# Expert 1's rows stay on the chip and its weights head SyncE's queue: a change to an mLSTM-and-routing kernel

## The chip, the cores and the metric

The kernel runs on one core of one Trainium2 chip. What counts is the device time of one execution in microseconds, as the median of several runs. Engines are named as in the profile: PE (TensorE matmul), PEld (its weight load), DVE (VectorE), ACT (ScalarE), POOL (GpSimd), SP (SyncE). SPq and POOLq are the DMA instructions that these engines issue; q1 is the DMA queue of SP's transfers, q0 that of POOL's.

## The reference

Two blocks follow each other. The first is an mLSTM cell over 4 batches, 8 heads, 768 time steps and head size 40. The second takes the result as 3072 rows of 320 numbers and sends each row through one of 8 experts, chosen by a hash of its token id:

```
for t in range(S):
    m_new = max(f_gate[t] + m, i_gate[t])
    f_stab, i_stab = exp(f_gate[t] + m - m_new), exp(i_gate[t] - m_new)
    C = f_stab * C + i_stab * outer(v[t], k[t]);  n = f_stab * n + i_stab * k[t]
    y[t] = sigmoid(o_gate[t]) * (C @ q[t]) / max(|n . q[t]|, 1)
x = y.transpose(0, 2, 1, 3).reshape(3072, 320)
expert_idx = token_ids * 2654435761 % 8
for e in range(8):
    rows = expert_idx == e
    out[rows] = relu(x[rows] @ w1[e]) @ w2[e]      # w1 320x1024, w2 1024x320
```

All data is float32.

## The kernel before, in words

**Attention stage** (until about 129 us). The 24 blocks of 128 rows are worked one after the other (the loop over `s`, L873). Meanwhile the routing tables are built: `g_idx` holds, for every expert, the numbers of the rows that it takes, `s_idx` where its results go. Each finished block of x is stored to a DRAM table `x_rows` (L585), the last ones from POOL's queue. Expert 0's weights are loaded in slices on SP's queue during the last blocks (`slices_of`, L120).

**Expert stage.** An expert takes 384 rows in three blocks (j = 0, 1, 2) and 32 remaining rows, 416 columns once turned. Its rows are gathered from `x_rows` by POOL's indirect DMA (`gather`, L109), turned so that the 320 features lie on partitions (`xT`: three blocks of features, the last one 64 wide and put there twice), multiplied by w1 with relu into `h` (layer 1) and by w2 into the result (layer 2), which ACT copies out of PSUM and POOL scatters to `out` (L980 to L993). The weights of one expert are `w1t` (256 x 1024), `w1c` (the last 64 rows of w1, folded) and `w2t`; `load_weights` (L116) issues them as four DMAs on SP.

*Expert 0* is written out plainly. `early_turn` (L807) turns its blocks 0 and 1 within the attention stage, and `layer1` (L142) makes h for these 256 columns at L970, in four rounds with two relus each: one on DVE (L165), one on ACT (L167). In the expert loop, `layer2` (L1107) follows for j = 0 and 1; between them PE turns the third block, `xg0[:, 2]` (`turn_third`), and inside j = 1 the remaining rows of experts 0 to 3 together, `xr0` (`turn_rest`). `turn` (L995) is two transposes, a 64-wide copy on DVE that doubles the last features (the pad, L1000), a third transpose, and a copy out of PSUM. Then layer 1 runs for the last 160 columns and layer 2 for j = 2.

*Experts 1 to 7* save one product in eight by sums: `sums_of_w1` (four DVE operations, `sw`), `sums_of_x` (`tx`), `differences_of_w2` (`tw`, on POOL), `sums_of_h` (`sh`). `layer1_by_seven` (PE lines L1060 and L1068) and `layer2_by_seven` (L1144) use them. Their rows are turned without PE: `fetch` gathers them into `xg`, SP writes that tile to a DRAM table `x_slots` (L1191; the remaining rows of four experts at L1198), `blocks` reads it back in twelve DMAs as 32-wide pieces (`xb`, L1206), and one DVE operation transposes the 32 x 32 squares (`turned`, L1210).

**What sets the order.** Every engine works its instructions in the order in which they are written, and so does SP's queue. Before the expert loop stand `fetch(0)`, `fetch(1)`, `blocks(1)`, `load_weights(1)`; in round e come `fetch(e+2)`, `blocks(e+2)`, `load_weights(e+2)` first. `sums_of_w1(W[e+1])` stands behind layer 2 of j = 2, for expert 0 too. The expert stage's tiles lie in memory that the attention stage's pools give back, so their first users wait for the last users of the old tiles.

Of the kernel before, what the change touches and what calls it, by code (L numbers as in the profile page):

```python
# [17 lines left out]
P = 128  # L18
# [4 lines left out]
def kernel(  # L23
# [85 lines left out]
    def gather(xg, idx, rows=N):  # L109
        nc.gpsimd.indirect_dma_start(  # L110
            out=xg, out_offset=None, in_=x_d[:rows, :], in_offset=bass.IndirectOffsetOnAxis(ap=idx, axis=0),
        )

    W = {}

    def load_weights(e, eng=None):  # L116

        W[e] = weights(moe_w1[e], moe_w2[e], wpools[e % 3 > 0], w2pools[e % 6 > 0], eng)
# [72 lines left out]
    with tc.tile_pool(name="gates", bufs=1) as gp, \  # L191
# [210 lines left out]
        def turn(s, what, tag="tr"):  # L402
            turned_in(s, what, tag)
            turned_out(s, what)
# [401 lines left out]

        def early_turn(j):  # L807
            tp = ps.tile([P, DB, P], F32, name="tpx", tag="tr", bufs=2)
            for db in range(DB):
                nc.tensor.transpose(tp[:, db, :], xg0[:, j, db * P : (db + 1) * P], ident[:])  # L810
            nc.scalar.copy(xT0[:, :, j * P : (j + 1) * P], tp[:])

        def unread(n):
# [59 lines left out]
        for s in range(NT):  # L873
# [76 lines left out]
                for j in range(2):  # L950
                    gather(xg0[:, j, :Dm], g_idx[:, j : j + 1], TE * P)
            if s == NT - 2:
                for j in range(2):
                    nc.vector.tensor_copy(xg0[:, j, Dm:], xg0[:, j, 2 * P : Dm])
                early_turn(0)
            if s == 2:
                g1.weights(kwT1)
# [19 lines left out]
    def psum():  # L977
        return mps.tile([P, 4 * P], F32, name="mh", bufs=8)
# [13 lines left out]
            tc.declare_no_dep(ins, group="rows_out", reason="disjoint rows")  # L992
            tc.add_to_no_dep_group("rows_out", ins)  # L993

    def turn(xg, dst, on_act):  # L995

        tp = psum().rearrange("p (d c) -> p d c", c=P)[:, :DB]
        for db in range(2):
            nc.tensor.transpose(tp[:, db, :], xg[:, db * P : (db + 1) * P], ident[:])
        nc.vector.tensor_copy(xg[:, Dm:], xg[:, 2 * P : Dm])  # L1000
        nc.tensor.transpose(tp[:, 2, :], xg[:, 2 * P :], ident[:])
        if on_act:
            nc.scalar.copy(dst, tp[:])
        else:
            nc.vector.tensor_copy(dst, tp[:])
# [169 lines left out]
    def cols_of(t, c0):  # L1175
        return lambda j: t[:, c0 + j : c0 + j + 1]

    with tc.manual_schedule():
        xTs, hrem, xbs = {}, {}, {}
        xr0 = xp.tile([P, DB * P], F32, name="xr0", bufs=1)  # L1180
        xTs[0] = xT0

        def fetch(e):
            if e == 0:
                gather(xg0[:, 2, :Dm], cols_of(g_idx, 0)(2))
                gather(xr0[:, :Dm], cols_of(g_idx, NR)(0))
            else:
                xg = xp.tile([P, NJ, Dm], F32, name="xg")
                for j in range(NJ):
                    gather(xg[:, j], cols_of(g_idx, e * NJ)(j))  # L1190
                nc.sync.dma_start(xs_d[e, :NM].rearrange("(t p) d -> p t d", p=P), xg[:])  # L1191
            if e % EG == 0:
                if e:
                    xr = xp.tile([P, Dm], F32, name="xrg", bufs=1)
                    gather(xr[:], cols_of(g_idx, NR + e // EG)(0))
                else:
                    xr = xr0[:, :Dm]
                nc.sync.dma_start(xs_d[e : e + EG, NM:], xr[:])  # L1198

        def blocks(e):  # L1200
            xb = xbs[e] = xp.tile([P, CAP // 32, DB, 32], F32, name="xb")
            rows = xs_d[e].rearrange("(g j) d -> j g d", j=32)
            for q in range(4):
                for c in range(DB):
                    d0 = c * P + (q if c + 1 < DB else q % 2) * 32
                    nc.sync.dma_start(xb[q * 32 : (q + 1) * 32, :, c], rows[:, :, d0 : d0 + 32])  # L1206
# [5 lines left out]
        def turn_third():  # L1212
            turn(xg0[:, 2], xT0[:, :, 2 * P : NM], False)

        def turn_rest():
            remT = xp.tile([P, DB, P], F32, name="remT", bufs=1)
            turn(xr0, remT[:], True)
            nc.gpsimd.tensor_copy(xT0[:, :, NM:], remT[:, :, :RM])

        def rest(g):  # L1220
            zp = psum()[:, :Dm]
# [5 lines left out]
                    )  # L1227
            scatter(zp, cols_of(s_idx, NR + g)(0), True)

        fetch(0)  # L1230
        fetch(1)
        blocks(1)
        load_weights(1)
        h = h0
        for e in range(E):
            g, i = e // EG, e % EG
# [4 lines left out]
            if i == 0:  # L1241
                hrem[g] = xp.tile([P, EG, FB, RM], F32, name="hrem")
            if e == 0:
                layer2(W[0], h, range(2), cols_of(s_idx, 0), True, lambda j: j == 0 and turn_third(), lambda j, fb: (j, fb) == (1, FB - 3) and turn_rest())
                layer1(W[0], xT0, h, 2 * P, CAP, bank)
                turned(1)
                tx = sums_of_x(xTs[1])
            else:
                tw = differences_of_w2(W[e])
                sh = xp.tile([P, 4, FB // 2, P], F32, name="sh", bufs=1)  # L1250
                layer1_by_seven(
                    W[e], sw, xTs[e], tx, h, lambda: 2 < e < E - 1 and turned(e + 1),
                    lambda g: sums_of_h(h, sh, g, nc.vector if g else nc.gpsimd),
                )
            nc.gpsimd.tensor_copy(hrem[g][:, i], h[:, :, NM:])
            layer2(W[e], h, (2,), cols_of(s_idx, e * NJ), True)
            if e + 1 < E:
                sw = sums_of_w1(W[e + 1])
            if i == EG - 1 and e + 1 < E:
                rest(g)  # L1260
# [62 lines left out]
```

## Time and profile before

| | |
|---|---|
| median of 3 runs | 354.02 us (353.84 to 356.44) |
| the profiled execution, its own time | 357.09 us |
| its span, from the first to the last profiled instruction | 355.3 us |
| mean granted TensorE clock | 0.98 |
| attention stage ends on PE | about 128.7 us |
| expert 0 ends on PE | about 159.0 us |
| expert 7's last PE work | about 345 us |
| HBM read and written | 46.28 MB and 12.38 MB |

A timeline row gives start, length, engine, line, operation, output<-inputs and a count; the bracket at its end is how long the engine stood idle before it and what ended that. A row of the windows view gives, for a stretch of time, its length, the busy time of PE, PEld, DVE, ACT and POOL, then the granted clock of PE (1.00 is full), the share of the DMA engines that was busy, and GB/s. Ends of PE rows are modelled, since matmuls overlap: a row's start to the next row's start is the better measure.

### The profile page before, as it was taken

How to read it: one execution, taken by the hardware profiler on the slowest of the kernel's cores; microseconds unless marked ns; L12 is line 12 of the kernel's file. 1: busy time of each engine (PE TensorE's matmuls, PEld its weight loads, DVE VectorE, ACT ScalarE, POOL GpSimd, SP SyncE). 2: the span in 40 equal slices, each digit the busy share in tenths (PEclk: the TensorE clock that was granted, in tenths of full speed). 3: DMA queues.
4: the chain of work that ended last, by engine and by line, in shares of the span. 5: the costliest groups of instructions: out<-in, count | busy, mean ns of one | idle time of the engine just before them, and what ended most of it. 6: DMA issues, size and time to landing. Idle time of an engine off the chain costs nothing.

```text
span 355.3 us, 10242 instructions
## 1 busy us (share of the span) xinstructions
PE 334.2 (94%) x4051; PEld 292.7 (82%) x4051; DVE 231.3 (65%) x542; ACT 130.0 (37%) x325; POOL 205.0 (58%) x316
## 2 busy tenths in 40 slices
PE   7799699999999899996999999999999999999993
PEld 6577588999988786766989899859989989899891
DVE  8977899888787851144576697745684785765610
ACT  4478656676656521110421411411321411411410
POOL 9562487987865317307444965942963946618512
PEclk9789999999999999998999999999999999999999
DMA  6599989898889974588697958768368477001001
GB/s 129 97 183 189 166 181 201 172 184 166 160 176 217 241 277 116 146 209 286 132 310 128 333 151 209 273 134 277 129 126 298 123 178 233 2 17 39 0 19 43
DMA packets 162871, 59.06 MB, mean 166 GB/s; under 512 B 140647, under 2 KB 158595, under 8 KB 162790
## 3 DMA queue, kind: packets, MB, share of 16 engines
q1 hardware_dynamic: 158854, 48.82, 59.5%
q0 software_dynamic: 2832, 9.34, 8.0%
q8 instruction: 33, 0.54, 0.6%
q10 hardware_dynamic: 1134, 0.21, 0.3%
q14 instruction: 18, 0.15, 0.1%
HBM read 46.28 MB, written 12.38 MB: 165 GB/s over the span
## 4 chain that ended last, share of the span: by engine, by line
PE 67%; DMA 9%; issue 6%; DVE 6%; POOL 6%; SPq 4%; ACT 1%; POOLq 0%; ACTq 0%; DVEq 0%
PE mh L1060 17%; PE mh L1144 13%; PE mh L1111 7%; PE xh L553 7%; PE mh L1068 5%; PE sp L480 5%; PE tr L413 4%; DMA og<-in_o_gate_dram 2%; DMA w1t<-in_moe_w_dram 2%; DMA x_slots<-xg 2%; SPq L1206 2%; PE ab L438 1%; PE xh L532 1%; PE mh L1224 1%; POOL out_dram L986 1%
## 5 line engine op out<-in xcount | busy, mean ns | idle before, releaser
L986 POOL DMA_INDIRECT out_dram<-zo,s_idx x26 | 26.5, 1021 | 71.2 <-issue 35.6
L1111 PE MATMUL mh<-w2t,h 128*128 128x320 f32 x160 | 45.0, 433 | 0.5 <-ACT h L167 0.5
L1111 PEld LDWEIGHTS mh<-w2t,h 128*128 128x128 f32 x160 | 30.0, 190 | 11.8 <-ACT h L167 0.9
L1046 DVE TENSOR_TENSOR h<-u,mh 128x416 f32<-128x416 f32 (+1 forms) x56 | 25.2, 476 | 17.0 <-PE mh L1068 6.2
L1060 PE MATMUL mh<-tx,sw 128*128 128x208 f32 x168 | 33.6, 352 | 1.0 <-DVE sw L1016 1.0
L1060 PEld LDWEIGHTS mh<-tx,sw 128*128 128x128 f32 x168 | 31.3, 199 | 1.4 <-DVE sw L1016 1.3
L110 POOL DMA_INDIRECT xg<-x_rows,g_idx x24 | 23.8, 990 | 13.0 <-issue 6.7
L1046 DVE TENSOR_TENSOR u<-m,mh 128x416 f32<-128x416 f32 x28 | 16.5, 588 | 19.7 <-PE mh L1060 16.5
L553 PE MATMUL xh<-v,w 128*64 128x41 f32 x384 | 27.5, 234 | 0.0
L1144 PE MATMUL mh<-tw,sh 128*128 128x160 f32 x168 | 27.4, 299 | 0.0
L496 DVE TENSOR_TENSOR w<-sp,w 128x384 f32<-128x384 f32 x48 | 24.5, 549 | 3.6 <-ACT w L442 3.6
L553 PEld LDWEIGHTS xh<-v,w 128*64 128x64 f32 x384 | 26.1, 145 | 0.0
L1060 PE MATMUL mh<-xT,w1t 128*128 128x208 f32 x112 | 23.2, 340 | 2.6 <-DMA w1t<-in_moe_w_dram 2.6
L480 PEld LDWEIGHTS sp<-qT,kT 40*64 40x64 f32 x960 | 20.2, 137 | 6.4 <-issue 5.0
L480 PE MATMUL sp<-qT,kT 40*64 40x64 f32 (+1 forms) x960 | 23.9, 238 | 1.6 <-issue 0.9
L1144 PEld LDWEIGHTS mh<-tw,sh 128*128 128x128 f32 x168 | 24.3, 190 | 0.0
L442 ACT ACTIVATE w<-ab 128x384 f32<-128x384 f32 x48 | 21.3, 488 | 5.4 <-PE ab L441 5.0
L1074 ACT COPY m<-mh 128x416 f32<-128x416 f32 x14 | 7.1, 505 | 42.9 <-PE mh L1060 34.2
L1060 PEld LDWEIGHTS mh<-xT,w1t 128*128 128x128 f32 x112 | 19.7, 190 | 3.0 <-issue 3.0
L1068 PE MATMUL mh<-xT,w1c 64*128 64x208 f32 x224 | 21.6, 342 | 0.0
L553 PE MATMUL xh<-vd,w 128*64 128x82 f32 x192 | 21.1, 251 | 0.5 <-ACT vd L506 0.5
L982 ACT COPY zo<-mh 128x320 f32<-128x320 f32 x12 | 5.1, 425 | 44.5 <-PE mh L1111 27.3
(267 smaller groups left out, 843.8 us busy)
## 6 DMA issues: line engine op xcount, KB each, us to landing
w2t<-in_moe_w_dram SPq DMA_DIRECT2D x7, 1280.0 KB
w1t<-in_moe_w_dram SPq DMA_DIRECT2D x7, 1024.0 KB
xb<-x_slots SPq DMA_DIRECT2D x84, 52.0 KB
k<-in_k_dram SPq DMA_DIRECT2D x24, 160.0 KB
v<-in_v_dram SPq DMA_DIRECT2D x24, 160.0 KB
og<-in_o_gate_dram SPq DMA_DIRECT2D x24, 160.0 KB
q<-in_q_dram SPq DMA_DIRECT2D x23, 160.0 KB
x_slots<-xg SPq DMA_DIRECT2D x7, 480.0 KB
```

The source lines that it names most:

```text
L110: nc.gpsimd.indirect_dma_start(out=xg, out_offset=None, in_=x_d[:rows, :], in_offset=bass.IndirectOffsetOnAxis(ap=idx, axis=0),)
L413: nc.tensor.transpose(tp[:DR, j, :], d[what][:, 2 * j : 2 * j + 2, :].rearrange("p h d -> p (h d)")[:, :DR], ident[:],)
L442: nc.scalar.activation(w[:, hf], ab, AF.Exp)
L480: nc.tensor.matmul(sp[hf][o * HB : (o + 1) * HB, m, bs], lhsT=kT[r, 2 * m + j, i], rhs=qT[r, 2 * m + j, ts], start=True, stop=True,)
L496: nc.vector.tensor_tensor(d["w"][:, hf], d["sp"][hf], d["w"][:, hf], op=ALU.mult)
L553: nc.tensor.matmul(xh[half[i], hs], lhsT=lhsT, rhs=rhs, start=first[i], stop=last, skip_group_check=True)
L986: ins = nc.gpsimd.indirect_dma_start(out=out[:, :], out_offset=bass.IndirectOffsetOnAxis(ap=idx, axis=0), in_=zo[:], in_offset=None, bound ...
L1046: nc.vector.tensor_tensor(o, a, b, op=ALU.add)
L1060: nc.tensor.matmul(pair(bank[n])[:, a], lhsT=lhsT(g + a), rhs=rhs, start=first and a == 0, stop=True, skip_group_check=True,)
L1068: nc.tensor.matmul(pair(bank[n])[:, a], lhsT=w1c[k, g + a, :], rhs=xT[k, 2, r], start=False, stop=True, skip_group_check=True,)
L1111: nc.tensor.matmul(zp, lhsT=h[:, fb, j * P : (j + 1) * P], rhs=w[2][:, fb, :], start=(fb == 0), stop=(fb == FB - 1),)
L1144: nc.tensor.matmul(bank[n], lhsT=lhsT(f), rhs=rhs(f), start=first and f == 0, stop=f == FB // 2 - 1, skip_group_check=True,)
```

## The change

Three things are moved and one is replaced.

- `load_weights(1)` stands first, ahead of `fetch(0)` and `fetch(1)`.
- Expert 1's gathered rows go to a tile of their own, `xg1`, are not written to `x_slots`, and `blocks(1)` and `turned(1)` are gone. Instead `turn_second` turns them on PE, nine transposes and three ACT copies behind layer 1 of expert 0's third part; the 32 remaining rows come from `remT`, already turned, by a POOL copy.
- `sums_of_w1(W[1])` stands between `turn_third` and layer 2 of j = 1, no longer behind layer 2 of j = 2.
- `padded` and `turns` are split out of `turn` and `early_turn`, so that one DVE copy can pad several blocks.

```diff
+    def padded(xg):
+        nc.vector.tensor_copy(xg[..., Dm:], xg[..., 2 * P : Dm])
+    def turns(tp, xg):
+        for db in range(2):
+            nc.tensor.transpose(tp[:, db, :], xg[:, db * P : (db + 1) * P], ident[:])
+        nc.tensor.transpose(tp[:, 2, :], xg[:, 2 * P :], ident[:])
...
-    def turn(xg, dst, on_act):
-
+    def turn(xg, dst, on_act, pad=True):
+
+        if pad:
+            padded(xg)
         tp = psum().rearrange("p (d c) -> p d c", c=P)[:, :DB]
-        for db in range(2):
-            nc.tensor.transpose(tp[:, db, :], xg[:, db * P : (db + 1) * P], ident[:])
-        nc.vector.tensor_copy(xg[:, Dm:], xg[:, 2 * P : Dm])
-        nc.tensor.transpose(tp[:, 2, :], xg[:, 2 * P :], ident[:])
+        turns(tp, xg)
...
+        xg1 = xp.tile([P, NJ, DB * P], F32, name="xg1", bufs=1)
+        remT = xp.tile([P, DB, P], F32, name="remT", bufs=1)
...
+            elif e == 1:
+                for j in range(NJ):
+                    gather(xg1[:, j, :Dm], cols_of(g_idx, e * NJ)(j))
...
+        def turn_second():
+            xT = xTs[1] = xp.tile([P, DB, CAP], F32, name="xT")
+            nc.gpsimd.tensor_copy(xT[:, :, NM:], remT[:, :, RM : 2 * RM])
+            for j in range(NJ):
+                turn(xg1[:, j], xT[:, :, j * P : (j + 1) * P], True, False)
...
+        load_weights(1)
         fetch(0)
         fetch(1)
-        blocks(1)
-        load_weights(1)
...
             if e == 0:
-                layer2(W[0], h, range(2), cols_of(s_idx, 0), True, lambda j: j == 0 and turn_third(), lambda j, fb: (j, fb) == (1, FB - 3) and turn_rest())
+                layer2(W[0], h, (0,), cols_of(s_idx, 0), True)
+                turn_third()
+                sw = sums_of_w1(W[1])
+                layer2(W[0], h, (1,), cols_of(s_idx, 0), True, within=lambda j, fb: fb == FB - 3 and turn_rest())
+                padded(xg1[:])
                 layer1(W[0], xT0, h, 2 * P, CAP, bank)
-                turned(1)
+                turn_second()
                 tx = sums_of_x(xTs[1])
...
-            if e + 1 < E:
+            if 0 < e < E - 1:
                 sw = sums_of_w1(W[e + 1])
```

How this moves the instructions shows at two places. On SP's queue, from expert 0's last weight slices (`w1t`, `w2t` at the top) to expert 2's transfers, before and now:

```order
L138 DMA w2t<-in_moe_w_dram 128x2x320 x4
L1276 TENSOR_LOAD xe
L1276 ISA x2
L1198 DMA x_slots<-xr_3065 4x32x320
L1191 DMA x_slots<-xg 128x3x320
L1206 DMA xb<-x_slots 32x13x32 x12
L97 DMA w1t<-in_moe_w_dram 128x2x1024
L100 DMA w1c<-in_moe_w_dram 64x4x128 x2
L101 DMA w2t<-in_moe_w_dram 128x8x320
```

```order
L148 DMA w2t<-in_moe_w_dram 128x2x320 x4
L97 DMA w1t<-in_moe_w_dram 128x2x1024
L100 DMA w1c<-in_moe_w_dram 64x4x128 x2
L101 DMA w2t<-in_moe_w_dram 128x8x320
L1210 DMA x_slots<-xr_3064 4x32x320
L1203 DMA x_slots<-xg 128x3x320
L1296 TENSOR_LOAD xe
L1296 ISA x2
L1218 DMA xb<-x_slots 32x13x32 x12
```

Expert 1's weights (L97 to L101) now follow expert 0's directly, and the `x_slots<-xg` and `xb` rows that are left are expert 2's.

On DVE, from the pad of expert 0's third block (`xg_72` is `xg0`, `h_74` is `h0`, `xT_73` is `xT0`) to the sums for expert 1, before and now:

```order
L1000 COPY xg_72<-xg_72 128x64
L165 TENSOR_SCALAR h_74<-mh_3026 128x256
L165 TENSOR_SCALAR h_74<-mh_3036 128x256
L1005 COPY xT_73<-mh 128x3x128
L1000 COPY xr_3065<-xr_3065 128x64
L165 TENSOR_SCALAR h_74<-mh 128x160 x4
L1210 STREAM_TRANSPOSE xT<-xb 128x13x3x32
L1021 TENSOR_TENSOR tx<-xT 128x208
L1022 TENSOR_TENSOR tx<-xT,tx 128x208
L1023 TENSOR_TENSOR tx<-xT 128x208
L1024 TENSOR_TENSOR tx<-xT,tx 128x208
L1014 TENSOR_TENSOR sw<-w1t 128x512
```

```order
L116 COPY xg_72<-xg_72 128x64
L175 TENSOR_SCALAR h_74<-mh_3025 128x256
L175 TENSOR_SCALAR h_74<-mh_3035 128x256
L1012 COPY xT_73<-mh 128x3x128
L1021 TENSOR_TENSOR sw<-w1t 128x512
L1022 TENSOR_TENSOR sw<-w1t 128x512
L1023 TENSOR_TENSOR sw<-sw,w1t 128x512
L1024 TENSOR_TENSOR sw<-w1t,sw 128x512
L116 COPY xr_3064<-xr_3064 128x64
L116 COPY xg_3065<-xg_3065 128x3x64
L175 TENSOR_SCALAR h_74<-mh 128x160 x4
L1028 TENSOR_TENSOR tx<-xT 128x208
```

The pad of `xg0` keeps its place ahead of the last two relus of the first layer-1 part; the four `sw` rows now stand ahead of the pad of `xr`, and the big transpose is gone.

More of the change, by code (lines that the diff above doesn't have):

```diff
@@ L808, in early_turn @@
             tp = ps.tile([P, DB, P], F32, name="tpx", tag="tr", bufs=2)
-            for db in range(DB):
-                nc.tensor.transpose(tp[:, db, :], xg0[:, j, db * P : (db + 1) * P], ident[:])
+            turns(tp, xg0[:, j])
             nc.scalar.copy(xT0[:, :, j * P : (j + 1) * P], tp[:])
@@ L952 @@
             if s == NT - 2:
-                for j in range(2):
-                    nc.vector.tensor_copy(xg0[:, j, Dm:], xg0[:, j, 2 * P : Dm])
+                padded(xg0[:, :2])
                 early_turn(0)
@@ L1215, in turn_rest @@
         def turn_rest():
-            remT = xp.tile([P, DB, P], F32, name="remT", bufs=1)
             turn(xr0, remT[:], True)
             nc.gpsimd.tensor_copy(xT0[:, :, NM:], remT[:, :, :RM])
+        def turn_second():
[3 more added lines that the diff above has]
+                turn(xg1[:, j], xT[:, :, j * P : (j + 1) * P], True, False)
         def rest(g):
```

## The prediction

> **What bounds the kernel now.** I read the page's busy times and chain first, then the PE timeline around the first two experts, then DVE, POOL and the DMA queues there.
>
> ```profile
> PE 334.2 (94%) x4051; PEld 292.7 (82%) x4051; DVE 231.3 (65%) x542; ACT 130.0 (37%) x325; POOL 205.0 (58%) x316
> PE 67%; DMA 9%; issue 6%; DVE 6%; POOL 6%; SPq 4%; ACT 1%; POOLq 0%; ACTq 0%; DVEq 0%
> ...
> 176.00:340.00 164.00, 163.84 (x1071) 148.60 (x1070) 107.24 (x203) 41.26 (x99) 96.51 (x92) 1.00 0.58 164
> ```
>
> The third row is one stretch of the windows view: from 176 to 340 us PE is busy 163.84 of 164 us. Nothing that the change hurries in that stretch can be gained; it only moves earlier or later as a block. So the change is worth what it does to PE before 176. The PE timeline there:
>
> ```profile
> 138.87 4.57 PE L1111 MATMUL mh<-w2t,h 128*128 128x320 f32 x16 [0.47 <-ACT h L167]
> 143.28 0.38 PE L999 MATMUL mh<-ident,xg 128*128 128x128 f32 x2
> 143.61 3.40 PE L1111 MATMUL mh<-w2t,h 128*128 128x320 f32 x12
> 147.06 0.27 PE L1001 MATMUL mh<-ident,xr 128*128 128x128 f32 x1
> ...
> 154.56 4.47 PE L1111 MATMUL mh<-w2t,h 128*128 128x320 f32 x16
> 161.58 0.94 PE L1060 MATMUL mh<-xT,w1t 128*128 128x208 f32 x4 [2.56 <-DMA w1t<-in_moe_w_dram]
> 163.55 4.06 PE L1060 MATMUL mh<-tx,sw 128*128 128x208 f32 x12 [1.02 <-DVE sw L1016]
> ...
> 171.75 3.08 PE L1068 MATMUL mh<-xT,w1c 64*128 64x208 f32 x32
> ...
> 189.60 0.87 PE L1060 MATMUL mh<-xT,w1t 128*128 128x208 f32 x4
> ...
> 196.73 3.08 PE L1068 MATMUL mh<-xT,w1c 64*128 64x208 f32 x32
> ```
>
> Expert 0 ends at 159.03 (154.56 + 4.47); expert 1 waits 2.56 us for its w1 and 1.02 us for the w1 sums. The same piece of work, L1060's start to L1068's, takes 10.17 us in expert 1 (161.58 to 171.75) and 7.13 us in expert 2 (189.60 to 196.73): 3.04 us more, 1.02 of it the sums, the other 2.02 a slow clock. The windows view, stretches of 3.4 us, second number PE busy, then PEclk near the end:
>
> ```profile
> 156.80:160.20 3.40, 2.23 (x9) 1.24 (x7) 2.46 (x5) 0.43 (x1) 0.43 (x1) 1.00 1.01 350
> 160.20:163.60 3.40, 0.99 (x5) 0.70 (x5) 2.06 (x4) 0.51 (x1) 2.79 (x3) 1.00 1.09 309
> 163.60:167.00 3.40, 3.40 (x10) 3.32 (x11) 1.54 (x3) 0.00 (x0) 1.98 (x3) 0.51 1.06 397
> ```
>
> After a stretch with 2.4 us idle PE ran the next at 0.51; after one with 1.2 us idle it did not. So the late load of expert 1 costs 2.56 + 3.04 = 5.6 us in all. Why it is late: the chain and SP's queue.
>
> ```profile
> 154.68 6.77 DMA w1t<-in_moe_w_dram
> ...
> 142.84 0.37 SPq L1191 DMA_DIRECT2D x_slots<-xg  x1
> ...
> 148.58 6.05 SPq L1206 DMA_DIRECT2D xb<-x_slots  x12
> ```
>
> The weights stand behind a round trip through DRAM and twelve issues.
>
> **The change part by part.** (1) Expert 1's load moves ahead on SP, and x_slots<-xg and twelve xb issues of expert 1 go away. In the built program the load now waits for the last attention matmul, whose memory it takes over. DVE's first step behind that matmul is the first row here; the others, of the DVE, ACT and POOL timelines, are used below:
>
> ```profile
> 128.81 0.17 DVE L571 TENSOR_SCALAR den<-xh 128x8 f32<-128x8 f32 x1 [0.73 <-PE xh L553]
> ...
> 136.11 0.20 DVE L1000 COPY xg<-xg 128x64 f32<-128x64 f32 x1 [2.83 <-DMA xg<-x_rows,g_idx]
> 136.22 0.42 DVE L165 TENSOR_SCALAR h<-mh 128x256 f32<-128x256 f32 x1
> ...
> 144.70 0.56 DVE L1005 COPY xT<-mh 128x384 f32<-128x384 f32 x1 [6.71 <-PE mh L1001]
> 145.39 0.26 DVE L1000 COPY xr<-xr 128x64 f32<-128x64 f32 x1
> ...
> 161.47 0.69 DVE L1014 TENSOR_TENSOR sw<-w1t 128x512 f32<-128x512 f32 x1 [2.15 <-DMA w1t<-in_moe_w_dram]
> ...
> 163.53 0.69 DVE L1017 TENSOR_TENSOR sw<-w1t,sw 128x512 f32<-128x512 f32 x1
> ...
> 138.43 0.38 ACT L167 ACTIVATE h<-mh 128x256 f32<-128x256 f32 x1 [1.94 <-issue]
> ...
> 147.37 0.48 ACT L1003 COPY remT<-mh 128x384 f32<-128x384 f32 x1 [2.23 <-PE mh L1001]
> ...
> 130.81 0.54 POOL L585 DMA_DIRECT2D x_rows<-x  x1 [1.90 <-DVE x L578]
> ...
> 133.13 1.00 POOL L110 DMA_INDIRECT xg<-x_rows,g_idx  x1 [1.78 <-DMA x_rows<-x]
> ```
>
> So the load is issued from about 128.8 instead of 154.68, 25.9 us earlier, and w1t lands near 135.6 (6.77 later). The waits for w1t and for the sums go, and the slow clock with them: **-5.6 us**.
>
> (2) Nine transposes are added to PE between L168's third part and the last layer 2 of expert 0. Three of them with what goes with them cost 0.33 us (143.28 to 143.61), so three groups **+1.0 us**. Behind them come three ACT copies (0.48 each) and four sums of x; in place of DVE's big transpose. The last copy ends some 1.5 to 2 us after the transposes, the four sums take about 1.5 more, and layer 2's 4.47 us cover that with about 1 us left. The 64-wide pad of three row blocks and one more POOL copy of 32 columns lie under the third part of layer 1. If that cover failed, PE would wait the missing part, 1 us at most by these rows; I take 0.
>
> (3) The load moves past something that matters more: POOL's last x store (130.81) and the gather of xg0's third block (133.13). Both now run while expert 1's weights stream, 1280 + 1024 + 2 x 128 KB by the page's DMA issues:
>
> ```profile
> w2t<-in_moe_w_dram SPq DMA_DIRECT2D x7, 1280.0 KB
> w1t<-in_moe_w_dram SPq DMA_DIRECT2D x7, 1024.0 KB
> ...
> x_slots<-xg SPq DMA_DIRECT2D x7, 480.0 KB
> ```
>
>  DVE's pad of that block stands ahead of the last two relus of the first layer-1 part, and layer 2's first matmul (138.87) waits for both relus. Today the gather lands at 136.11, the relus end 0.11 + 0.42 + 0.42 = 0.95 later on DVE, at 137.06 at the earliest, and ACT's relu, ending at 138.81, comes last. The slack is 1.75 us: once the gather lands after 137.86, PE waits. What a weight stream does to POOL's transfers is seen once before, when the scatter of 159.77 and three gathers met expert 1's weights; these rows are the DMA view of 159.8 to 163.8 (the first two) and of 163.8 to 168.5 (the other two), then POOL's last gather there:
>
> ```profile
> DMA packets 1080, 1.21 MB, mean 303 GB/s; under 512 B 20, under 2 KB 1079, under 8 KB 1080
> q1 hardware_dynamic: 1080, 1.21, 108.8%
> ...
> q1 hardware_dynamic: 572, 0.69, 41.2%
> q0 software_dynamic: 192, 0.66, 34.7%
> ...
> 159.77 0.98 POOL L986 DMA_INDIRECT out_dram<-zo,s_idx  x1 [4.25 <-ACT zo L982]
> ...
> 163.91 1.12 POOL L110 DMA_INDIRECT xg<-x_rows,g_idx  x1 [0.30 <-issue]
> ```
>
> In the first four microseconds every one of the 1080 packets is SP's (q1); POOL's queue q0 has none, though its scatter was issued at 159.77. All four POOL transfers (0.66 MB) move after 163.8 and are done by 168.5. So under the stream a POOL transfer takes at least 4.0 us to its first packet, about 5.0 with its data, and the last gather 4.6 (163.91 to 168.5). Alone, the store takes 2.3 (130.81 to 133.13) and the gather 3.0 (133.13 to 136.11). By these prices store and gather lose 2.7 + 1.6 = 4.3 us, the gather lands at 140.4, and layer 2 starts at 140.4 + 0.95 = 141.4, a wait of 2.5 us. The bounds: 0, if the transfers share fairly; and 4.9, if the store gets nothing until the whole load is through. About 0.2 MB of that load was left at 163.8 (q1's 0.69 MB less the 0.48 of x_slots), so it ends 9.7 us after its issue, here at 138.5; store about 139.5, gather 3.3 later at 142.8, layer 2 at 143.75. I take **+3.0**, near the analogy but above it, since the store comes 2 us behind the load's start where the scatter came 5 us behind it.
>
> (4) Clock. A wait of 3.0 beside the 0.47 of today leaves PE idle from 138.4 to 141.9: 1.4 us in the stretch that ends at 139.8 and 2.1 us in the next. The rows above halve the clock after 2.4 and not after 1.2. I take one halved stretch, half of 3.4: **+1.7** (bounds 0 and 3.4). The Trainium skill, "TensorE: Matmul & The Clock Gate" (Part 1), puts re-throttling behind a whole idle window of about 3.4 us; by it a wait of 3 us would not halve the clock and this term would be 0. This trace halved it after less, so the rows decide.
>
> (5) The w1 sums now stand on DVE ahead of the pad of xr, which the third transpose of the remaining rows (147.06) waits for. From the copy's start at 144.70: 0.69 to the next step, the sums 2.75 (161.47 to 164.22), the pad 0.26, so 148.4 against 147.06: 1.3 us late. If the copy starts as soon as its transposes end (143.8), 0.4. With PE at half clock DVE has more time. I take **+0.4**, bounds 0 and 1.3. Behind the sums on DVE wait only the third part's relus, which come after.
>
> Sum: -5.6 + 1.0 + 3.0 + 1.7 + 0.4 = **+0.5 us**. On the profiled execution, 357.09 us with a span of 355.3, that is 357.6; the median of the runs, 354.02, lies 3.1 lower, so I forecast 354.5.
>
> **The rivals.** *Fair sharing (A).* The store and the gather get their turns among the weights, the gather lands before 137.86, PE does not wait: -5.6 + 1.0 + 0.4 = -4.2, 349.8 us (350.7 with 1.3 for the sums). For it: one store and one gather are small against the stream. Against it: the empty q0 above. The Trainium skill states this rule: in "DMA: Bandwidth & Descriptors" (Queues, rings and completion order) each engine goes round-robin between queues, a packet at a time. The four microseconds without a q0 packet do not look like it.
>
> *Behind the whole load (B), the slower case.* The store's packets come after all of the load: a wait of 4.9, two halved stretches (3.4) and 1.3 for the sums: -5.6 + 1.0 + 4.9 + 3.4 + 1.3 = +5.0, 359.0 us. It decides from a pad start past 142. For it: q0 moved nothing until the weights were nearly through; against it: the store is issued while only part of the load can be queued.
>
> *Wait without slow clock (C).* As forecast but without the 1.7: -1.2, 352.8 us. It turns on how 2.1 us idle is judged between 1.2 and 2.4.
>
> *The load does not start early (D).* If SP holds it until its queue moved on before, about 138.8, w1t lands at 145.6, the sums end at 148.35 and the pad at 148.6, 1.5 late: -5.6 + 1.0 + 1.5 = -3.1, 350.9 us. Against it: what it waits for ended by 128.8.
>
> **How the numbers follow.** Forecast 0.45, A 0.22, C 0.15, B 0.13, D 0.05. A measurement of this kernel tells about 1% (3.5 us) from no change: below 350.5 is faster, above 357.6 slower. Faster takes most of A and a little of C and D, 0.19; slower nearly all of B and a tail of the forecast, 0.14; the rest, 0.67, is within 1%. The range goes from 350.2, inside A, to 357.8, short of B, which leaves about 2 in 10 out.
>
> **What would show it.** DVE's pad of xg0's third block at 139 to 142 instead of 136.11, and an idle of 2 to 4 us before expert 0's first layer 2, with relus on DVE as its end: step 3. A half clock just behind it: step 4. No idle before expert 1's first L1067 row and 7.1 us from there to L1075: step 1. A pad that starts before 138 makes A right; one past 142, B. If w1t lands after 140, step 1's issue time is wrong; if PE waits ahead of expert 1 for tx, step 2's cover is.

## The result and the profile after

| | median us | runs | lowest to highest |
|---|---|---|---|
| before | 354.94 | 17 | 350.63 to 360.65 |
| with the change | 358.90 | 17 | 355.49 to 361.44 |

The ratio is 1.0139 with a 95% interval of 1.0103 to 1.0174: slower by 1.4%. The profiled execution took 358.57 us, its span 356.5. Ratios, here and below, leave out runs over 1.5% above the fastest of their kernel, which drops 7 of before's 17 runs but one of the change's, so medians over all runs stand beside them: by these the change is 1.1% slower (4.0 us).

The PE timeline of the change, in the places that the prediction showed of before:

```profile
143.32 6.38 PE L1118 MATMUL mh<-w2t,h 128*128 128x320 f32 x16 [5.18 <-issue]
...
153.72 0.33 PE L122 MATMUL mh<-ident,xr 128*128 128x128 f32 x1 [0.24 <-DVE xr L116]
...
161.28 0.38 PE L121 MATMUL mh<-ident,xg 128*128 128x128 f32 x2
...
162.26 4.47 PE L1118 MATMUL mh<-w2t,h 128*128 128x320 f32 x16
166.57 0.87 PE L1067 MATMUL mh<-xT,w1t 128*128 128x208 f32 x4
...
173.69 2.56 PE L1075 MATMUL mh<-xT,w1c 64*128 64x208 f32 x26
```

Expert 1 begins with no wait, and from L1067 to L1075 are 7.12 us: what the change was for has happened. But the first layer 2 of expert 0 starts at 143.32 after 5.18 us idle, where before had 138.87 after 0.47. The SP, POOL and DVE timelines say why (the issue of expert 1's first weights, the last store of x, the gather of the third block, its pad, the relus behind it, and the later pad of xr):

```profile
128.66 0.37 SPq L97 DMA_DIRECT2D w1t<-in_moe_w_dram  x1
...
130.56 0.54 POOL L595 DMA_DIRECT2D x_rows<-x  x1 [2.37 <-DVE x L588]
138.40 1.00 POOL L110 DMA_INDIRECT xg<-x_rows,g_idx  x1 [7.30 <-PE mh L168]
...
142.37 0.20 DVE L116 COPY xg<-xg 128x64 f32<-128x64 f32 x1 [9.34 <-DMA xg<-x_rows,g_idx]
142.47 0.75 DVE L175 TENSOR_SCALAR h<-mh 128x256 f32<-128x256 f32 x2
...
153.48 0.19 DVE L116 COPY xr<-xr 128x64 f32<-128x64 f32 x1
```

From store to gather pass 7.84 us (2.32 before), from gather to pad 3.97 (2.98 before). The row of 138.40 names PE as what ended the 7.30, but L168 had run for long: the store's landing at 138.14 is what came, as the trace's DMA events show. The windows view of the change, in stretches of 3.4 us (PE busy second, PEclk third from the end):

```profile
136.80:140.20 3.40, 1.34 (x7) 0.84 (x5) 0.00 (x0) 0.38 (x1) 1.50 (x2) 1.00 0.70 230
140.20:143.60 3.40, 0.28 (x1) 0.31 (x2) 0.86 (x3) 0.00 (x0) 2.49 (x4) 0.50 0.53 143
143.60:147.00 3.40, 3.40 (x7) 2.22 (x7) 0.00 (x0) 0.00 (x0) 2.72 (x3) 0.50 0.52 137
```

Two stretches ran at 0.50; the first row block of layer 2 took 6.22 us (143.32 to 149.54) for before's 4.41.

One stretch of the program holds nearly all that differs. I call it **the middle**: from the start of the last eight matmuls of the first layer 1 (136.40 in before's first profile, 136.15 in the change's) to the start of L1068, now L1075. It took 35.35 us in the profile that the prediction used and 37.54 in the change, +2.19. What follows it took 182.8 to 183.5 us in every profile below; what goes ahead of it varies by execution.

### The profile page after: what moved, and what is told of

It reads as the page before. It is cut to its first block, busy times and chain, and to the rows that moved or that the text cites. A ratio compares the mean times of both kernels' runs of the same rounds, so it can differ in the third digit from the quotient of the medians.

```text
span 356.5 us, 10250 instructions
## 1 busy us (share of the span) xinstructions
PE 336.0 (94%) x4060; PEld 295.0 (83%) x4060; DVE 229.2 (64%) x541; ACT 131.5 (37%) x328; POOL 204.8 (57%) x317
## 4 chain that ended last, share of the span: by engine, by line
PE 71%; DVE 7%; issue 7%; POOL 6%; DMA 4%; SPq 2%; ACT 1%; POOLq 0%; DVEq 0%; ACTq 0%
PE mh L1067 14%; PE mh L1151 13%; PE mh L1118 9%; PE xh L563 8%; PE sp L490 5%; PE tr L423 5%; PE mh L1075 4%; PE mh L168 3%; PE xh L542 2%; POOL xg L110 2%; POOL out_dram L994 2%; PE ab L448 1%; PE mh L1241 1%; DMA x_slots<-xrg 1%; DMA xrg<-x_rows,g_idx 1%
## 5 line engine op out<-in xcount | busy, mean ns | idle before, releaser
L1118 PE MATMUL mh<-w2t,h 128*128 128x320 f32 x160 | 46.8, 446 | 5.2 <-issue 5.2
L1118 PEld LDWEIGHTS mh<-w2t,h 128*128 128x128 f32 x160 | 31.1, 197 | 17.2 <-issue 6.7
L1067 PE MATMUL mh<-tx,sw 128*128 128x208 f32 x168 | 31.8, 339 | 0.0
L1067 PEld LDWEIGHTS mh<-tx,sw 128*128 128x128 f32 x168 | 29.7, 190 | 0.0
L563 PE MATMUL xh<-v,w 128*64 128x41 f32 x384 | 28.3, 238 | 0.0
L563 PEld LDWEIGHTS xh<-v,w 128*64 128x64 f32 x384 | 26.9, 149 | 0.0
L1067 PE MATMUL mh<-xT,w1t 128*128 128x208 f32 x112 | 23.1, 339 | 0.0
L1075 PE MATMUL mh<-xT,w1c 64*128 64x208 f32 x224 | 21.6, 342 | 0.0
L1151 PE MATMUL mh<-w2t,h 128*128 128x160 f32 x112 | 21.0, 300 | 0.0
L1075 PEld LDWEIGHTS mh<-xT,w1c 64*128 64x128 f32 x224 | 19.3, 187 | 1.8 <-issue 1.8
```

The source lines that it names most:

```text
L563: nc.tensor.matmul(xh[half[i], hs], lhsT=lhsT, rhs=rhs, start=first[i], stop=last, skip_group_check=True)
L1067: nc.tensor.matmul(pair(bank[n])[:, a], lhsT=lhsT(g + a), rhs=rhs, start=first and a == 0, stop=True, skip_group_check=True,)
L1075: nc.tensor.matmul(pair(bank[n])[:, a], lhsT=w1c[k, g + a, :], rhs=xT[k, 2, r], start=False, stop=True, skip_group_check=True,)
L1118: nc.tensor.matmul(zp, lhsT=h[:, fb, j * P : (j + 1) * P], rhs=w[2][:, fb, :], start=(fb == 0), stop=(fb == FB - 1),)
L1151: nc.tensor.matmul(bank[n], lhsT=lhsT(f), rhs=rhs(f), start=first and f == 0, stop=f == FB // 2 - 1, skip_group_check=True,)
```

## The experiments

"Expert 1" below is the stretch from the last layer-2 block of expert 0 to L1068, at least 11.4 us (162.26 to 173.69 above); what goes over that is lost there.

### Before and the change, profiled again

> The kernel before, unchanged, for a second profile. The runs of before lie in two heaps, near 350.7 and near 355 to 357, and the profiled one (357.1) is of the upper heap. If the 5.6 us at expert 1 belong to every run, L1060's start to L1068's takes 10.2 us here too, whatever the time; if the halved clock there is what parts the heaps, a run near 350.7 shows 7 to 8 us and no clock of 0.51 there.

> The kernel before, unchanged, for a third profile. From L1060's start to L1068's took 10.17 us in the first (with a wait of 2.56 ahead and a clock of 0.51) and 8.49 in the second (wait 1.21, full clock). If the first was the exception, this one has about 8.2 to 8.5 and a wait of 1 to 2 us: step 1 of the prediction is then worth 2.5 to 3.5 us in most runs, not 5.6.

> The kernel before, unchanged, for a fourth profile: the stretch from the last layer-2 block of expert 0 to L1068's start took 17.2, 14.2 and 12.3 us where 11.4 is the least. A value near 12 to 14 makes the first profile's 17.2 the exception and puts the usual gain of the early load at 1 to 3 us; another near 17 puts it nearer to 4.

> The change, unchanged, for a second profile. If its first one is usual, the pad of the third block is within 0.6 us of w2t's landing, PE starts layer 2 4 to 5.2 us after the end of layer 1, a stretch of 3.4 to 6.8 us at 0.5 follows, and 356 to 360 us in all. If the wait was an exception it is 3 or less, and the time below 356.

PE rows of before's second, third and fourth profile, one fence each:

```profile
153.22 4.47 PE L1111 MATMUL mh<-w2t,h 128*128 128x320 f32 x16
158.90 0.94 PE L1060 MATMUL mh<-xT,w1t 128*128 128x208 f32 x4 [1.21 <-DMA w1t<-in_moe_w_dram]
160.86 2.38 PE L1060 MATMUL mh<-tx,sw 128*128 128x208 f32 x12 [1.02 <-DVE sw L1016]
```

```profile
153.52 4.47 PE L1111 MATMUL mh<-w2t,h 128*128 128x320 f32 x16
157.83 0.87 PE L1060 MATMUL mh<-xT,w1t 128*128 128x208 f32 x4
159.26 2.38 PE L1060 MATMUL mh<-tx,sw 128*128 128x208 f32 x12 [0.56 <-DVE sw L1016]
```

```profile
153.33 4.47 PE L1111 MATMUL mh<-w2t,h 128*128 128x320 f32 x16
158.67 0.94 PE L1060 MATMUL mh<-xT,w1t 128*128 128x208 f32 x4 [0.87 <-DMA w1t<-in_moe_w_dram]
160.65 2.38 PE L1060 MATMUL mh<-tx,sw 128*128 128x208 f32 x12 [1.03 <-DVE sw L1016]
```

None has a halved clock there. Expert 1 loses 5.8 us in the first profile (17.20 less 11.4) and 2.7, 0.8 and 2.4 in these: **2.9 on the mean**. The loss grows with the lateness of the load's issue: 0.12 us behind the start of that layer-2 block in the first profile, 0.49, 2.18 and 1.01 us ahead of it in the others (SP's L97 at 152.73, 151.34 and 152.32). These three took 352.52, 351.15 and 352.29 us: the profile that I priced was an expensive execution, and what made it so was in the term to be removed. Since these three lie below before's median of 354.94, though, 2.9 may be somewhat less than a middling execution loses.

The change's second profile, 358.50 us, repeats the first in kind: pad at 140.99, 1.4 us earlier, PE idle 4.44 us ahead of layer 2, then two stretches at half clock, and 7.44 us for the first row block.

```profile
140.99 0.20 DVE L116 COPY xg<-xg 128x64 f32<-128x64 f32 x1 [8.60 <-DMA xg<-x_rows,g_idx]
...
141.95 7.60 PE L1118 MATMUL mh<-w2t,h 128*128 128x320 f32 x16 [4.44 <-issue]
```

### The load alone

```diff
+        load_weights(1)
         fetch(0)
         fetch(1)
         blocks(1)
-        load_weights(1)
```

> The kernel before with one edit: expert 1's weight load moves first on SP. The round trip, DVE's big turn and the place of the w1 sums stay. Theory (the late gather): the load's early start is the whole loss. The x store lands near 138.1 and the third block's gather near 142.3, DVE's pad of it stands ahead of the last two relus, PE starts expert 0's layer 2 near 143.3 after some 4.7 us idle, and part of that layer 2 runs at half clock (+1.8). Against it stands the 5.6 us at expert 1, so the time is that of the change less its nine transposes (1.0) and the sums ahead of xr's pad (0.4): ratio to before 1.000 to 1.010. Rival (the turn by TensorE and the moved sums cost the time, and the load is harmless): pad near 136 to 138, no idle before layer 2, ratio 0.984 to 0.988.

Median 356.27 against 354.29, ratio 1.0104 (1.0031 to 1.0178). The loss is there without any turn by TensorE and without moved sums:

```profile
141.93 0.20 DVE L1000 COPY xg<-xg 128x64 f32<-128x64 f32 x1 [9.50 <-DMA xg<-x_rows,g_idx]
...
142.89 6.02 PE L1111 MATMUL mh<-w2t,h 128*128 128x320 f32 x16 [5.35 <-issue]
```

The rival falls. The ratio lies just above the theory's 1.000 to 1.010, as it should if the 5.6 that it set against the loss is nearer to 2.9.

### The load kept, the pad behind the relus

```diff
         def turn_third():
-            turn(xg0[:, 2], xT0[:, :, 2 * P : NM], False)
+            with tc.issue_after(getattr(relus[FB // 2 - 1], "ins", relus[FB // 2 - 1])):
+                padded(xg0[:, 2])
+            turn(xg0[:, 2], xT0[:, :, 2 * P : NM], False, False)
```

> The change with one order changed on DVE: the pad of expert 0's third block stands behind the last two relus of the first layer 1 instead of ahead of them. The load stays first on SP, so store and gather are as late as in the change. Theory (the relus wait behind the pad): the gather still lands near 142.3, but layer 2 starts near 138.9, and only the third block's transposes, near 143.3, need the gather; no idle above 0.5, no half clock there; -5.6 + 1.0 + 0.4: ratio 0.985 to 0.992. Rival (PE, the relus' own inputs or the clock are held up by something else under the weight stream): layer 2 starts at 142 or later in this kernel too, ratio 1.00 to 1.014.

```profile
135.90 1.00 POOL L110 DMA_INDIRECT xg<-x_rows,g_idx  x1 [5.58 <-DMA x_rows<-x]
136.54 0.42 DVE L175 TENSOR_SCALAR h<-mh 128x256 f32<-128x256 f32 x1 [1.07 <-PE mh L168]
137.84 4.57 PE L1118 MATMUL mh<-w2t,h 128*128 128x320 f32 x16 [0.47 <-ACT h L177]
140.65 0.20 DVE L116 COPY xg<-xg 128x64 f32<-128x64 f32 x1 [3.69 <-DMA xg<-x_rows,g_idx]
```

Store and gather are late as ever (5.85 us from store to landing, 4.7 for the gather), the pad is at 140.65, and PE does not wait: the relus went ahead of it. Median 352.20, ratio 0.9989 (0.9949 to 1.0030) where the change has 1.0139: one order on DVE makes up for the loss, so it is the pad's place ahead of the relus through which the late gather costs time. The ratio falls short of the forecast, since by the profiles only 2.9 less 1.0 and 0.4 can be had; the medians of all runs lie 2.1 us apart.

### The load behind the first gathers, with the sums late and early

```diff
-        load_weights(1)
         fetch(0)
+        load_weights(1)
         fetch(1)
...
                 turn_third()
-                sw = sums_of_w1(W[1])
                 layer2(W[0], h, (1,), ...)
                 padded(xg1[:])
+                sw = sums_of_w1(W[1])
```

> The change with two statements moved: expert 1's load stands behind x_slots<-xr on SP, which waits for the gather of xr, so that the x store and the first two gathers run alone; and the w1 sums stand behind the pads of xr and xg1 on DVE. Theory (the late gather): pad of the third block near 136.1, layer 2 of expert 0 starts near 138.9 without idle, w1t is issued near 138 and lands near 145, in time for the sums; no wait at expert 1. What is left is -5.6 + 1.0 (nine transposes): ratio 0.985 to 0.990. Rival (the turn by TensorE and the moved sums cost the time): the loss of the change stays, ratio 1.00 to 1.014.

```profile
135.32 0.20 DVE L116 COPY xg<-xg 128x64 f32<-128x64 f32 x1 [3.00 <-DMA xg<-x_rows,g_idx]
...
137.91 4.57 PE L1118 MATMUL mh<-w2t,h 128*128 128x320 f32 x16 [0.47 <-ACT h L177]
...
147.22 0.69 DVE L1021 TENSOR_TENSOR sw<-w1t 128x512 f32<-128x512 f32 x1 [3.21 <-DMA w1t<-in_moe_w_dram]
```

The rows are as the theory has them: gather alone in 2.9 us, no idle, no wait at expert 1. Only w1t landed later than it says, at 147.20, still in time. Median 352.58; ratio 0.9992 (0.9947 to 1.0038), again less gain than forecast, for the same reason. With only the first half of the edit, the sums ahead of the pads:

> The change with expert 1's load behind x_slots<-xr on SP, as in the earlier kernel, but the w1 sums left ahead of the pads of xr and xg1 on DVE. w1t landed at 147.2 there, the sums ended at 149.9. Theory (what stands behind the sums on DVE waits for w1t): the pad of xr is near 149.9 instead of 143.6, the third transpose of the remaining rows comes 3.5 to 4 us late, PE waits that long inside layer 2's second block, perhaps with one halved stretch (1.7 more): ratio 1.005 to 1.015, against 0.999 with the sums behind the pads. Rival (the place of the sums does not matter): within 0.003 of that kernel.

```profile
148.89 0.69 DVE L1021 TENSOR_TENSOR sw<-w1t 128x512 f32<-128x512 f32 x1 [4.39 <-DMA xg<-x_rows,g_idx]
...
151.55 0.19 DVE L116 COPY xr<-xr 128x64 f32<-128x64 f32 x1
...
151.80 0.48 PE L122 MATMUL mh<-ident,xr 128*128 128x128 f32 x1 [4.50 <-DVE xr L116]
```

Ratio 1.0168 (1.0092 to 1.0244), median 359.16: the sums wait for w1t (landed 148.77), xr's pad for the sums, PE for the pad, and two stretches run at half clock. So the place of the sums costs the change as little as 0.45 us because its load is so early.

### Half the load ahead of the store

```diff
-        load_weights(1)
+        load_weights(1, True)
         fetch(0)
+        W[1] = *W[1][:2], w2_of(1)
         fetch(1)
```

Here w1t and w1c are loaded first and w2t behind x_slots<-xr.

> The change with expert 1's w2t issued behind x_slots<-xr on SP, so that only w1t and w1c (1.28 MB of 2.56) stream ahead of the store and the gather. Theory (transfers land in the order in which they were issued, whichever queue they came by): the x store lands with the second w1c as in the change, 5.9 to 7.6 us after its issue, but the gather behind it has no w2t ahead and takes 2.9 to 3.3 us instead of 3.9 to 4.7; pad 0.8 to 1.4 us earlier on the clock than in the change, near 141, wait 3.3 to 4.0 instead of 4.7; ratio to before 1.005 to 1.012. Rival (a fixed delay of software transfers beside hardware ones): the store lands as late as in the change and the gather still takes 3.9 or more.

```profile
135.96 1.00 POOL L111 DMA_INDIRECT xg<-x_rows,g_idx  x1 [5.11 <-DMA x_rows<-x]
...
138.98 0.20 DVE L117 COPY xg<-xg 128x64 f32<-128x64 f32 x1 [6.21 <-DMA xg<-x_rows,g_idx]
...
139.94 4.54 PE L1124 MATMUL mh<-w2t,h 128*128 128x320 f32 x16 [2.05 <-issue]
...
149.63 0.33 PE L123 MATMUL mh<-ident,xr 128*128 128x128 f32 x1 [1.37 <-DVE xr L117]
```

The store still took 5.4 us, the gather 3.0 as alone. The wait is 2.05, shorter than expected because w1 came in faster too (its last part landed at 136.01, in the change at 138.76); no stretch was halved. PE waited another 1.37 us for the pad of xr, which stands behind the sums on DVE. Ratio 1.0082 (1.0042 to 1.0123). In the change, then, the store pays for w1 and the gather for w2t.

### Is it the idle time that halves the clock?

```diff
+                un = psum()
+                for _ in range(40):
+                    nc.tensor.matmul(un[:, :P], lhsT=ident[:], rhs=ident[:], start=True, stop=True)
                 layer2(W[0], h, (0,), cols_of(s_idx, 0), True)
```

> The change with 40 matmuls of 128x128 that nobody reads (they compute nothing of the output) on PE ahead of expert 0's first layer 2: they take about 4.6 us and fill the wait of 4.7. Theory (idle time of PE brings the halved clock): the wait for the relus stays, the third block's pad is near 142, but no stretch between 137 and 150 us runs at 0.5, and the first row block of layer 2 takes 4.4 to 4.6 us instead of 6.22: 1.8 us less than the change, ratio to before 1.006 to 1.010. Rival (the halved clock comes by itself or from the weight stream): the row block takes 6 us or more again.

This try tells nothing of the question. Its bank (the PSUM buffer that the unread matmuls write) came free only with the late relus, so the unread matmuls stood behind the wait (PE idle 3.41 us, `[3.41 <-DVE h L175]`), and they took 12.0 us, not 4.6: ratio 1.0356 (1.0303 to 1.0410). In the second try they stand ahead of the wait, in a bank that is free:

```diff
             hp = [bank(i) for i in range(2)]
+            for _ in range(fill if 2 * (fp + 1) == FB else 0):
+                nc.tensor.matmul(hp[0][:, :P], lhsT=ident[:], rhs=ident[:], start=True, stop=True)
```

> The change with 18 matmuls of 128x128 that nobody reads (they compute nothing of the output) in the last quarter of the first layer 1, ahead of its own matmuls, in its own bank, so that they wait for nothing new. By the earlier try, 40 of them took 8.6 us at full clock; 18 take 3.9 us and end the first layer 1 near 142.0 instead of 138.1. Theory (idle time of PE brings the halved clock): the pad stays near 140.5 to 142.4, PE is idle at most 1.5 us before layer 2, no stretch between 138 and 150 us runs at 0.5, and the first row block of layer 2 takes 4.4 to 4.6 us instead of 6.22; ratio to before 1.004 to 1.011, some 1.8 us under the change. Rival (the weight stream, not the idle time, brings the halved clock): a stretch at 0.5 between 138 and 150 us again, row block 5.9 or more, ratio 1.012 or more.

```profile
133.47 4.29 PE L158 MATMUL mh<-ident 128*128 128x128 f32 x36
...
139.41 0.20 DVE L116 COPY xg<-xg 128x64 f32<-128x64 f32 x1 [8.64 <-DMA xg<-x_rows,g_idx]
...
140.78 4.58 PE L1120 MATMUL mh<-w2t,h 128*128 128x320 f32 x16 [0.47 <-ACT h L179]
```

With the same stream and the gather as late as ever behind the load's issue, but PE busy until the relus, the clock stayed at 1.00 and the row block took 4.41 us (140.78 to 145.19). So PE's idle time, not the weight stream, brought the halved clock. Median 356.57, ratio 1.0101 (1.0038 to 1.0165): as expected, but its interval overlaps the change's, so it is the granted clock and the row block that show this, not the time.

### Can the early load be had without the nine transposes?

Before with the load first and the pad late (the two edits above), and the round trip kept:

> The kernel before with two edits: expert 1's load first on SP, and DVE's pad of expert 0's third block behind the last two relus of the first layer 1. No turn by TensorE for expert 1, no moved sums. Theory (the late gather costs only through the relus behind the pad): the gather lands some 0.4 us behind w2t, near 141 to 142, but layer 2 of expert 0 starts without idle; no wait at expert 1, whose rows come by the old round trip in time as they did with the load alone. All of the gain is kept: -2.7 (second profile of before) to -5.6 (first) against before: ratio 0.986 to 0.992, about 1.0 us (0.3%) under the kernel with the pad late and the turn by TensorE. Rival (the early load has a second price that the earlier runs hid): ratio 0.998 or more, with a wait of over 1 us on PE somewhere between 137 and 166 us.

> The kernel with the load first and the pad late, on the old round trip, unchanged, for a second profile: in the first ACT's copy of the remaining rows started at 150.08 though its transposes ended near 147.4, POOL's copy waited for it and PE for POOL (2.49 us, then a halved stretch). If this belongs to the kernel, the copy is late by over 2 us again and PE waits at the third part of layer 1; if it was one execution's own, PE does not wait there and the time is near 351.

None of the gain was kept: ratio 1.0073 (1.0030 to 1.0117), median 355.42 against 354.47. The rival holds, and the two profiles show two prices. The first (ACT's copy of xr, POOL's copy behind it, PE):

```profile
150.08 0.48 ACT L1004 COPY remT<-mh 128x384 f32<-128x384 f32 x1 [6.01 <-remote]
...
150.62 0.26 POOL L1222 COPY xT<-remT 128x96 f32<-128x96 f32 x1 [2.28 <-ACT remT L1004]
...
150.94 2.18 PE L158 MATMUL mh<-xT,w1t 128*128 128x160 f32 x8 [2.49 <-POOL xT L1222]
```

and the second, where that copy was in time and PE waited at expert 1 for sums that stand behind a late turn:

```profile
156.94 1.48 DVE L1211 STREAM_TRANSPOSE xT<-xb 128x1248 f32<-128x1248 f32 x1 [2.09 <-DMA xb<-x_slots]
...
161.79 2.38 PE L1061 MATMUL mh<-tx,sw 128*128 128x208 f32 x12 [1.75 <-DVE sw L1017]
```

The second profile, 353.42 us, had no wait at the third part, so the first one's was not in every execution; but it was not near 351 either. With the gathers late, POOL's queue and the round trip are late too: SP issued the first xb read 10.0 to 11.6 us behind the start of expert 0's layer 2, in before 7.3 to 9.7. In the load-alone kernel PE's own wait had hidden that: its xb reads were issued later still (from 151.03), but PE came to expert 1 only at 164.33. With w1 put between x_slots<-xg and the xb issues instead (`load_weights(1, True)` ahead of `blocks(1)`, w2t behind it):

> The kernel before with expert 1's w1t and w1c put between x_slots<-xg and the twelve xb issues on SP, and w2t behind them. No turn by TensorE, no moved sums. The x store, the third block's gather and xr's gather run ahead of any weight stream. By transfers that land in the order of their issue: w1t issued near 142 to 143, landed near 150; xb some 1 to 3 us later than in before, DVE's big turn near 156 to 157, layer 1 of expert 1 starts at once (159 on the first profile's clock); -0.8 to -5.8 against the profiles of before: ratio 0.988 to 0.996. Rival (the round trip suffers under the weights as the gathers did): xb ends after 159, PE waits 2 us or more ahead of expert 1, ratio 1.00 or more.

```profile
157.88 1.48 DVE L1216 STREAM_TRANSPOSE xT<-xb 128x1248 f32<-128x1248 f32 x1 [2.61 <-DMA xb<-x_slots]
...
162.73 4.06 PE L1066 MATMUL mh<-tx,sw 128*128 128x208 f32 x12 [2.27 <-DVE sw L1022]
```

Ratio 1.0119 (1.0048 to 1.0190), median 357.10 against 355.14: the rival's ratio, with a halved stretch on top. But xb was there by 157.88, not after 159, and PE began expert 1 at once; its 2.27 us came later, for sums that here too stand behind the turn. So the last two kernels, again with the load first and the pad late, move the sums ahead of the third part's relus; the second also gives POOL's copy to ACT:

```diff
+                sw = sums_of_w1(W[1])
                 layer1(W[0], xT0, h, 2 * P, CAP, bank)
                 turned(1)
...
-            nc.gpsimd.tensor_copy(xT0[:, :, NM:], remT[:, :, :RM])
+            nc.scalar.copy(xT0[:, :, NM:], remT[:, :, :RM])
```

> The kernel before with the load first, the pad late, and expert 1's w1 sums ahead of the third part's relus on DVE; the round trip and DVE's big turn stay. With the load first and the pad late alone, PE waited 1.75 us at expert 1 for the sums, which stood behind DVE's turn at 156.9. Theory (the early load's second price is only the place of the sums): the sums run near 145 to 148, DVE turns near 157, tx ends near 159.7, no wait over 0.5 at expert 1; the stretch from the last layer-2 block of expert 0 to L1069 takes 11.4 to 12.0 us (17.2, 14.2 and 12.3 in the three profiles of before); ratio to before 0.986 to 0.996. Rival (the round trip itself is too late under the weights): PE waits over 1 us for tx or at the third part of layer 1, ratio 1.00 or more.

> The same with the copy of the remaining rows into expert 0's block moved from POOL, where eight gathers and a scatter stand ahead of it, to ACT behind the copy that feeds it. Theory: POOL's copy ended 0.1 us ahead of PE's need, so in some executions PE waited for it (2.49 us in one of two); without it the upper runs go and the median falls by 0.5 to 1.5 us: ratio 0.984 to 0.994. Rival (it was ACT's late start, not POOL, that PE waited for): the same as with POOL's copy, within 0.002.

Medians 352.33 and 351.50 against 354.72; ratios 0.9967 (0.9930 to 1.0004) and **0.9935 (0.9893 to 0.9978)**. The first lies just outside its forecast of 0.986 to 0.996, and its interval includes 1. The second beats before and with it the change; their intervals do not tell the two apart, so what POOL's copy is worth stays open. What is left in the first is PE's 0.77 us for POOL's copy, in the second 1.25 for DVE's turn:

```profile
148.64 1.35 PE L158 MATMUL mh<-xT,w1t 128*128 128x160 f32 x8 [0.77 <-POOL xT L1222]
```

```profile
157.25 0.97 PE L1061 MATMUL mh<-xT,w1t 128*128 128x208 f32 x4 [1.25 <-DVE xT L1211]
```

### The kernels side by side

| kernel | PE idle ahead of layer 2 | lost at expert 1 | the middle | median, and before's beside it |
|---|---|---|---|---|
| before, four profiles | 0.47 | 5.8, 2.7, 0.8, 2.4 | 35.35, 32.33, 30.42, 32.00 | 354.94 |
| change, two profiles | 5.18, 4.44 | 0 | 37.54, 38.03 | 358.90 (354.94) |
| load alone | 5.35 | 0 | 35.91 | 356.27 (354.29) |
| change, pad late | 0.47 | 0 | 31.05 | 352.20 (354.29) |
| change, load and sums later | 0.47 | 0 | 30.58 | 352.58 (354.29) |
| change, load later only | 0.47 | 0 | 37.74 | 359.16 (355.14) |
| change, half the load first | 2.05 | 0 | 33.71 | 356.32 (354.47) |
| load first, pad late, two profiles | 0.47 | 0, 2.0 | 33.84, 31.61 | 355.42 (354.47) |
| w1 ahead of the xb reads | 0.47 | 4.2 | 33.81 | 357.10 (355.14) |
| load first, pad late, sums early | 0.47 | 0 | 30.55 | 352.33 (354.72) |
| the same, copy on ACT | 0.47 | 1.6 | 31.20 | 351.50 (354.72) |

The two kernels with unread matmuls are not in the table, since these lie in the middle or move its start.

## Why the prediction was wrong

The forecast was +0.5 us; the middle's means differ by 37.8 - 32.5 = **+5.3**, the medians by +4.0. Two terms of the sum failed by their size, not by their mechanism: the gain of step 1 was put too high, and the wait of step 3 with its slow clock, step 4, too low. Point by point:

- **Step 1, -5.6: the mechanism right, the size wrong.** The wait, the sums and the slow clock at expert 1 are gone in every profile of the change. But they are worth 2.9 us on the mean of four executions; the forecast took them from the one at hand. It had the sign of this before it: that execution lay 3.1 us over the median. It took those 3.1 off the result as a shift of the whole, when they sat in the very term that the change removes. On the means this is 2.7 us of the miss. At the median it is less: with the other steps as measured below, medians 4.0 apart leave step 1 a worth of about 4 us (an estimate).
- **Step 2, +1.0: right.** Nine transposes from 161.28 to 162.26 are 0.98, and PE does not wait for tx.
- **Step 3, +3.0: the place right, the size wrong.** PE waits for relus that stand behind the pad, and the pad for the gather. Beyond the usual 0.47 the wait is 4.7 and 4.0 us. The prices came from the scatter and gather of 159.77, which met a stream already five microseconds old; the text saw that the store comes much earlier and gave 0.5 us for it. The store took 7.6 and 6.5 us from issue to landing (2.1 to 3.1 in seven profiles without the load there), the gather 3.9 and 4.3 (2.9 to 3.0). The load also ran longer than the 9.7 us that the text worked out: from w1t's issue to w2t's last landing event 13.2 and 12.5 us in the change, and 11.4 in the very profile that it read (154.68 to 166.07).
- **Step 4, +1.7: 1.8 in the first profile, 3.0 in the second.** Two stretches were halved, not one; in the first profile PE sat idle through most of the first of them. Steps 3 and 4 together are 6.5 and 7.0 for 4.7: 1.8 to 2.3 us of the miss.
- **Step 5, +0.4: right**, 0.45 (L122's group took 0.78 us, from 153.10 to 153.88, for 0.33).

Set against the first profile of before, the terms measured give -5.8 + 1.0 + 4.7 + 1.8 + 0.45 = +2.2, which is the middle's difference. Against the mean of four, step 1 is -2.9 and the sum +5.

The case nearest to the result is the second rival (B), 359.0 us, with its two halved stretches. Its sign, a pad past 142, stands in the first profile (142.37) and not in the second (140.99). Its mechanism holds in half: the gather, not the store, ends behind the whole load. That its time is met within 0.1 us is luck: it took 5.6 for step 1, 3.4 for the clock and 1.3 for the sums, where the runs show some 3 to 4, 1.8 to 3.0 and 0.45. The rival of fair sharing (A) is out: PE waited in both profiles. So is the one without a slow clock (C): the stretch ahead of the halved ones had 2.05 us idle by its matmul records. So is the late load (D): the load was issued at 128.66, as step 1 said.

## What to carry to other kernels

A loss read from one profile is one draw. If that execution lies off the median, look for what it has more of before pricing a change that removes just that. And when a large load moves ahead on one queue, follow every small transfer of the other queues that now runs under it to the instruction that waits for it, and to what is queued behind that instruction: here a pad of 0.2 us ahead of two relus cost more than the load's early start gained, and moving the pad alone brought the ratio from 1.0139 to 0.9989.

## What was not expected of the hardware

**A transfer is as late as its slowest sixteenth.** Each of these transfers shows 16 landing events. In the change fifteen of the gather's came by 141.36 and the last at 142.34; w2t's last came at 141.91, when twelve of its sixteen had been in by 139.45 (the first at 138.90). In ten profiles with the whole load ahead of the gather, the gather's last event followed w2t's last recorded one by 0.42 to 0.45 us (in two of them some events are missing). The Trainium skill, "DMA: Bandwidth & Descriptors" (Why a DMA increments its semaphore by 16 and not by 1), says that only the full 16 mean that all data landed; the trace agrees. Strict order of issue does not hold, though: with the load behind the first gathers, a gather issued at 141.24 landed by 149.34, ahead of w2t, issued at 140.15 and landed at 152.71.

**In the expert stage, somewhat over half a stretch idle was enough to halve the clock.** Behind 130 us, in all profiles together and up to the last stretches of the program, PE was idle 2.05 us or more in eight stretches of 3.4 us at full clock (2.05, 2.27, 2.38, 2.49, 2.55, 2.96 and twice all of it); the next ran at half each time. In no stretch there with 1.77 us or less did that happen. The Trainium skill, "TensorE: Matmul & The Clock Gate" (Part 1), asks for a whole idle window; six of the eight were not. The limit is not one for all matmuls: in the attention stage, where they are smaller, the clock was halved after less. In before's first profile one stretch with 0.96 us idle was enough (the row's second number is PE busy, the third from the end the clock):

```profile
119.30:122.70 3.40, 2.44 (x65) 1.92 (x62) 2.29 (x9) 1.31 (x5) 2.72 (x5) 1.00 1.10 291
122.70:126.10 3.40, 3.40 (x50) 3.18 (x46) 2.78 (x7) 1.40 (x4) 0.56 (x1) 0.50 1.06 298
```

So recorded idle time alone does not tell when the clock is halved; no run here separates what else counts.

**Left open.** In the first profile of the kernel with load first and pad late, ACT's copy started 2.7 us after its transposes had been recorded as ended, with nothing else to wait for; PE's finishing signals came in a burst at 150.02. Before's third profile shows the same by 1.6 us, without cost. No run here shows the cause.
